# Lightning attention and a cosine FFN on one core: x produced transposed, state kept in PSUM with positional powers, FFN and attention interleaved in a fixed order

**Chip, cores, metric.** One core of one Trainium2 chip. The metric is the device time of one execution in microseconds (us), the median of several. The profile's span is some 1.7 us shorter than the device time of the same execution, so differences are taken within one of the two. The profiled execution of the kernel before is not among the three of its table: its span is 421.0. Lines with "..." mark cuts in code and in views.

## The reference

Two programs, one feeding the other. Attention with a decay lambda per head (4 batches, 8 heads, 768 positions, 64 features per head):

```python
for b in range(nb):                                   # blocks of 64 positions
    intra = (qb @ kb.T) * Dmask                       # Dmask[i,j] = lam**(i-j) for i >= j, else 0
    intra = intra @ vb
    inter = (qb * lam**(pos + 1)) @ kv_state
    out[block] = intra + inter
    kv_state = lam**block * kv_state + (kb * lam**(block-1-pos)).T @ vb
```

(That is the reference with its einsums written as products.) Then `x`, the output as 3072 tokens of 512 features, goes through an FFN with 2048 hidden features:

```python
h = x @ w_in
g = h * np.cos(h)
return (g @ w_out).astype(np.float32)
```

## The kernel before

It works in blocks of 128 tokens, 24 in all, and head by head. One head is a ring of small operations (cut to it):

```python
for h in range(H):
    ...
    ps_qkT = ps2_pool.tile([2 * D, BLK], BF16, tag="ps_qkT")
    nc.tensor.transpose(ps_qkT, qk_s[:, h, :, :], identb)
    ...
    nc.scalar.copy(q_b, ps_qkT[0:D, :])
    ...
    nc.vector.tensor_copy(k_b, ps_qkT[D:2 * D, :])
    ps_s = ps_pool.tile([BLK, BLK], F32, tag="ps_s")
    nc.tensor.matmul(ps_s, lhsT=k_b, rhs=q_b, start=True, stop=True)
    ...
    nc.vector.tensor_mul(s_masked, ps_s, dm_h)           # decay and causality in one mask per head
    ...
    nc.tensor.matmul(ps_o, lhsT=s_masked, rhs=v_sb, start=True, stop=first)
    if not first:
        nc.tensor.matmul(ps_o, lhsT=q_b, rhs=kv, start=False, stop=True)
    nc.scalar.copy(o_sb, ps_o)
    ...
    nc.tensor.matmul(ps_kv, lhsT=qk_s[:, h, 1, :], rhs=v_sb, start=True, stop=True)
    ...                                                  # new_kv = lam**128 * kv + ps_kv, two operations
nc.sync.dma_start(out=x_dram[r0:r0 + BLK, :], in_=o_all)
```

Only when attention is over does the FFN run, six tiles of 512 tokens, loading `x` back from memory and transposing it on PE:

```python
for t0 in range(0, N_TOK, T):
    for nt in range(NT):
        ...
        nc.sync.dma_start(out=x_tile, in_=x_dram[t0 + nt * 128:t0 + (nt + 1) * 128, :])
        for kd in range(KD):
            ...
            nc.tensor.transpose(ps_t, x_tile[:, kd * 128:(kd + 1) * 128], ident_bf)
            nc.scalar.copy(xT[:, kd, nt * 128:(nt + 1) * 128], ps_t)
    ...
    for f in range(KF):                                  # 16 slices of the hidden features
        ...                                              # 4 matmuls into ps_h, cosine on ACT, gate on DVE
        for nt in range(NT):                             # 4 matmuls that use the gate just made
            nc.tensor.matmul(out_ps[nt], lhsT=g[:, nt * 128:(nt + 1) * 128], rhs=w_out_sb[:, f, :], ...)
```

## Time and profile before

| | before |
|---|---|
| device time, median of 3 (range) | 419.84 (419.66 to 420.62) |
| span of the profile | 421.0 |
| busy: PE, DVE, ACT, POOL | 85%, 47%, 55%, 18% of the span |
| instructions | 6366 |
| first FFN matmul | 204.8 |

Added here is one turn of the attention's ring, from the timeline of the kernel before. Columns: start, length (us), engine, line, operation, output<-inputs, shapes; in brackets the idle time before it and what ended it.

```profile
60.56 0.23 DVE L136 COPY k_b<-ps_qkT 64x128 bf16<-64x128 bf16 x1
60.68 0.29 PE L139 MATMUL ps_s<-q_b,k_b 64*128 64x128 bf16 x1
61.01 0.29 DVE L141 TENSOR_TENSOR s_masked<-ps_s,dmaskT 128x128 bf16<-128x128 f32 x1 [0.23 <-PE ps_s L139]
```

Three operations of 0.23 to 0.29 us hand one head's 128x128 block from engine to engine. A matmul of 128 columns takes 0.29 us here because it is seen alone, from issue to landing. PE is "98% busy" in this stretch without ever streaming: the busy share of a latency-bound PE says little.

### The profile page before, as it was taken

The numbers are of one execution on the slowest core, as the hardware profiler recorded it, in microseconds if no ns is written. First come the engines' busy times: TensorE is split into PE (matmuls) and PEld (weight loads), VectorE is DVE, ScalarE is ACT, GpSimd is POOL, SyncE is SP. The second block draws the span as 40 slices with busy tenths as digits, with TensorE's granted clock in tenths as the row PEclk, the third lists the DMA queues.
The fourth block names the chain that finished last, engine by engine and source line by source line (L and its number), as shares of the span: only waits on it lengthen the run. The fifth ranks groups of instructions, "written<-read, shape, count | busy, mean of one in ns | idle before, by whom it ended". The sixth has DMA issues, their size and how long they took to land.

```text
span 421.0 us, 6366 instructions
## 1 busy us (share of the span) xinstructions
PE 356.0 (85%) x1792; PEld 169.1 (40%) x1792; DVE 196.4 (47%) x713; ACT 230.5 (55%) x796; POOL 75.3 (18%) x71
## 2 busy tenths in 40 slices
PE   0565999999999999994788888888888888888883
PEld 0232555555555555552334333433434343433331
DVE  4653777777777777773122323333232323232331
ACT  5544776777678767872633454363363445344323
POOL 5505643434343535200000000000000000000000
PEclk9999999999999999999999999999999999999998
DMA  9999947474647474201100030030011002002002
GB/s 165 214 194 227 213 107 158 106 159 102 138 101 160 104 154 111 62 19 47 50 14 12 13 126 12 12 114 26 12 64 63 25 19 107 15 0 100 0 2 100
DMA packets 88020, 36.07 MB, mean 86 GB/s; under 512 B 76208, under 2 KB 84400, under 8 KB 87984
## 3 DMA queue, kind: packets, MB, share of 16 engines
q1 hardware_dynamic: 85392, 31.47, 31.7%
q0 software_dynamic: 2592, 4.19, 5.4%
q8 instruction: 14, 0.23, 0.3%
q14 instruction: 22, 0.18, 0.1%
HBM read 30.41 MB, written 9.44 MB: 95 GB/s over the span
## 4 chain that ended last, share of the span: by engine, by line
PE 71%; ACT 9%; DVE 8%; issue 6%; POOL 3%; DMA 2%; ACTq 0%; SPq 0%; POOLq 0%
PE out_ps L192 22%; PE ps_h L185 11%; PE ps_qkT L132 9%; PE ps_o L145 9%; ACT cos_h L188 8%; PE ps_kv L152 8%; DVE g L190 8%; PE ps_o L147 6%; PE ps_s L139 5%; POOL qk_s L121 2%; DMA x_tile<-x_attn 1%; DMA lam_bc<-in_lam_dram 1%; PE ps_t L178 1%; DMA out_dram<-o_tile 0%; POOL dmaskT L80 0%
## 5 line engine op out<-in xcount | busy, mean ns | idle before, releaser
L190 DVE TENSOR_TENSOR g<-ps_h,cos_h 128x512 bf16<-128x512 f32 x96 | 66.4, 692 | 152.0 <-ACT cos_h L188 152.0
L188 ACT ACTIVATE cos_h<-ps_h,halfpi 128x512 f32<-128x512 f32 x96 | 66.0, 687 | 109.9 <-PE ps_h L185 109.8
L192 PE MATMUL out_ps<-w_out_sb,g 128*128 128x512 bf16 x384 | 100.5, 386 | 25.9 <-DVE g L190 25.9
L185 PE MATMUL ps_h<-xT,w_in_sb 128*128 128x512 bf16 x384 | 100.6, 386 | 0.0
L141 DVE TENSOR_TENSOR s_masked<-ps_s,dmaskT 128x128 bf16<-128x128 f32 x192 | 56.0, 292 | 49.8 <-PE ps_s L139 49.7
L132 PE MATMUL ps_qkT<-identb,qk_s 128*128 128x128 bf16 x192 | 55.0, 288 | 23.7 <-POOL qk_s L121 23.7
L134 ACT COPY q_b<-ps_qkT 64x128 bf16<-64x128 bf16 x192 | 49.6, 259 | 43.8 <-PE ps_qkT L132 27.8
L121 POOL TENSOR_TENSOR qk_s<-qk_f,qk_scale 128x1024 bf16<-128x1024 f32 x24 | 56.2, 2341 | 79.6 <-PE ps_kv L152 73.4
L192 PEld LDWEIGHTS <-g 128*128 128x128 bf16 x384 | 33.9, 99 | 72.8 <-DVE g L190 37.9
L185 PEld LDWEIGHTS <-w_in_sb 128*128 128x128 bf16 x384 | 38.1, 99 | 47.1 <-issue 3.2
L139 PE MATMUL ps_s<-q_b,k_b 64*128 64x128 bf16 x192 | 55.7, 290 | 0.1
L158 ACT ACTIVATE kv<-kv,lam_blk 64x64 bf16<-64x64 bf16 x160 | 55.5, 347 | 0.1
L152 PE MATMUL ps_kv<-v_all,qk_s 128*64 128x64 bf16 x192 | 49.9, 260 | 0.1
L149 ACT CAST o_all<-ps_o 128x64 bf16<-128x64 f32 x192 | 40.6, 211 | 12.6 <-PE ps_o L147 2.7
L145 PE MATMUL ps_o<-v_all,s_masked 128*128 128x64 bf16 x192 | 45.3, 236 | 1.5 <-DVE s_masked L141 1.2
L136 DVE COPY k_b<-ps_qkT 64x128 bf16<-64x128 bf16 x192 | 43.5, 226 | 6.3 <-ACT kv L158 0.2
L147 PE MATMUL ps_o<-kv,q_b 64*128 64x64 bf16 x160 | 37.1, 232 | 0.0
L152 PEld LDWEIGHTS <-qk_s 128*64 128x64 bf16 x192 | 24.2, 126 | 26.6 <-issue 0.2
L132 PEld LDWEIGHTS <-qk_s 128*128 128x128 bf16 x192 | 19.7, 103 | 36.0 <-POOL qk_s L121 23.8
L145 PEld LDWEIGHTS <-s_masked 128*128 128x128 bf16 x192 | 20.2, 105 | 32.4 <-DVE s_masked L141 32.3
L159 DVE TENSOR_TENSOR kv<-kv,ps_kv 64x64 bf16<-64x64 bf16 x160 | 32.4, 202 | 0.0
L179 ACT COPY xT<-ps_t 128x128 bf16<-128x128 bf16 x96 | 20.6, 268 | 6.8 <-PE ps_t L178 6.8
(37 smaller groups left out, 123.1 us busy)
## 6 DMA issues: line engine op xcount, KB each, us to landing
qk_f<-in_q_dram SPq DMA_DIRECT2D x24, 256.0 KB, 4.3
qk_f<-in_k_dram SPq DMA_DIRECT2D x24, 256.0 KB, 4.3
v_f<-in_v_dram SPq DMA_DIRECT2D x24, 256.0 KB, 4.0
out_dram<-o_tile SPq DMA_DIRECT2D x24, 256.0 KB, 2.0
x_attn<-o_all SPq DMA_DIRECT2D x24, 128.0 KB, 1.8
x_tile<-x_attn SPq DMA_DIRECT2D x24, 128.0 KB, 2.0
w_in_sb<-in_moe_w_in_dram POOLq DMA_DIRECT2D x1, 2048.0 KB, 14.2
w_out_sb<-in_moe_w_out_dram POOLq DMA_DIRECT2D x1, 2048.0 KB, 27.0
```

The source lines that it names most:

```text
L121: nc.gpsimd.tensor_mul(qk_s, qk_f, qk_scale)
L132: nc.tensor.transpose(ps_qkT, qk_s[:, h, :, :], identb)
L139: nc.tensor.matmul(ps_s, lhsT=k_b, rhs=q_b, start=True, stop=True)
L141: nc.vector.tensor_mul(s_masked, ps_s, dm_h)
L145: nc.tensor.matmul(ps_o, lhsT=s_masked, rhs=v_sb, start=True, stop=first)
L147: nc.tensor.matmul(ps_o, lhsT=q_b, rhs=kv, start=False, stop=True)
L152: nc.tensor.matmul(ps_kv, lhsT=qk_s[:, h, 1, :], rhs=v_sb, start=True, stop=True)
L158: nc.scalar.activation(new_kv, kv, AF.Copy, scale=lb_h[0:D, :])
L185: nc.tensor.matmul(ps_h, lhsT=w_in_sb[:, kd, f * 128:(f + 1) * 128], rhs=xT[:, kd, :], start=(kd == 0), stop=(kd == KD - 1))
L188: nc.scalar.activation(cos_h, ps_h, AF.Sin, bias=halfpi)
L190: nc.vector.tensor_mul(g, ps_h, cos_h)
L192: nc.tensor.matmul(out_ps[nt], lhsT=g[:, nt * 128:(nt + 1) * 128], rhs=w_out_sb[:, f, :], start=(f == 0), stop=(f == KF - 1))
```

## The change

The intent is that PE should have one continuous stream of work. Four things are done for it:

1. **Positional powers.** Rows of q are scaled by lambda^position and rows of v by lambda^-position, counted from the start of the batch. Then the mask is a plain triangle, the same for all heads, and the state needs no decay: it is a plain sum, left in one PSUM bank over the six blocks of a batch. (The lambdas of the test are 0.97 to 0.99, so lambda^-767 stays below 2e10; it grows as lambda falls.)
2. **Heads in pairs.** Two heads share each transpose (128 features), each score matmul (256 columns, q laid out block-diagonally) and each output; 8 heads' results move in one or two wide operations.
3. **x transposed on chip.** The value matmuls have their operands swapped, so that they give features x tokens, which the FFN reads as its `xT`. Two heads, each with v padded by zeros, add into one output. x is not stored or loaded.
4. **A fixed order.** Attention of tile i+1, first FFN matmuls of tile i and second FFN matmuls of tile i-1 share each of 16 slots of a stage; a block of attention is four slots.

The core of the diff, with cuts marked:

```diff
+    ctx.enter_context(tc.manual_schedule())
...
-                    nc.vector.tensor_mul(s_masked, ps_s, dm_h)
+        nc.vector.tensor_mul(s_m[n][:, 4 * half:4 * half + 4, :], sc.pop((n, half)),
+                             mask.unsqueeze(1).to_broadcast([P, 4, P]))
...
-                    nc.tensor.matmul(ps_o, lhsT=s_masked, rhs=v_sb, start=True, stop=first)
+        for p in range(NP):
+            if c:
+                nc.tensor.matmul(t[:, p, :], lhsT=kv_bd[(n - 1) % NK][:, p, :],
+                                 rhs=qkT[n][:, 0, p, :], start=True, stop=False)
+            for i in range(2):
+                nc.tensor.matmul(t[:, p, :], lhsT=v_pad[n % NV][:, 2 * p + i, :],
+                                 rhs=s_m[n][:, 2 * p + i, :],
+                                 start=(i == 0 and c == 0), stop=(i == 1))
...
-                        nc.scalar.activation(new_kv, kv, AF.Copy, scale=lb_h[0:D, :])
-                        nc.vector.tensor_add(new_kv, new_kv, ps_kv)
+            nc.tensor.matmul(kv_ps[:, p, :], lhsT=k_b[n][:, 2 * p:2 * p + 2, :],
+                             rhs=v_both(n, p), start=(c == 0 and p == 0), stop=True, ...)
...
-                nc.sync.dma_start(out=x_dram[r0:r0 + BLK, :], in_=o_all)
+        nc.scalar.copy(xT[i][:, :, j * P:(j + 1) * P], o_ps.pop(n))
...
+    for i in range(-1, NTILE + 1):
+        for s in range(KF):
+            ...                                    # weights in quarters, in stages -1 and 0
+            if 0 <= i < NTILE:
+                ffn_in(i, s)                       # 4 matmuls
+                ffn_cos(i, s)                      # ACT
+            after = None
+            if i + 1 < NTILE:
+                after = attend((i + 1) * NT + s // 4, s % 4)   # PE part of attention
+            if 0 <= i < NTILE:
+                ffn_gate(i, s)                     # DVE
+            if after:
+                after()                            # DVE or ACT part of attention
+            if i >= 1:
+                ffn_out(i - 1, s)                  # 4 matmuls
+                ffn_store(i - 1, s)
```

`attend` does the next block's transposes in slot 0, the first half of the scores and the state update in slot 1, the other half in slot 2, the values in slot 3.

## The prediction

> **What bounds the kernel now.** I read the windows view first, because the page averages over two programs run one after the other. Columns: the stretch, its length, busy time and instructions of PE, PEld, DVE, ACT, POOL, then clock, DMA share, GB/s.
>
> ```profile
> 15.00:34.00 19.00, 12.14 (x60) 6.13 (x60) 9.55 (x44) 9.28 (x40) 3.88 (x5) 1.00 1.16 200
> 34.00:196.00 162.00, 157.96 (x868) 81.58 (x868) 113.18 (x532) 117.20 (x504) 62.95 (x43) 1.00 0.57 122
> 196.00:205.00 9.00, 3.17 (x16) 1.54 (x17) 0.00 (x0) 3.04 (x14) 0.00 (x0) 1.00 0.25 78
> 205.00:414.00 209.00, 182.35 (x848) 79.90 (x847) 66.41 (x96) 91.46 (x200) 0.00 (x0) 1.00 0.11 38
> 414.00:421.00 7.00, 0.40 (x2) 0.00 (x0) 0.00 (x0) 2.04 (x4) 0.00 (x0) 0.84 0.40 150
> ```
>
> Some 34 us of start, 162 of attention, 9 of changeover, 209 of FFN, 7 of tail. Next the costliest groups, with the durations for pricing the change:
>
> ```profile
> L190 DVE TENSOR_TENSOR g<-ps_h,cos_h 128x512 bf16<-128x512 f32 x96 | 66.4, 692 | 152.0 <-ACT cos_h L188 152.0
> L188 ACT ACTIVATE cos_h<-ps_h,halfpi 128x512 f32<-128x512 f32 x96 | 66.0, 687 | 109.9 <-PE ps_h L185 109.8
> ...
> L192 PE MATMUL out_ps<-w_out_sb,g 128*128 128x512 bf16 x384 | 100.5, 386 | 25.9 <-DVE g L190 25.9
> ...
> L132 PE MATMUL ps_qkT<-identb,qk_s 128*128 128x128 bf16 x192 | 55.0, 288 | 23.7 <-POOL qk_s L121 23.7
> L134 ACT COPY q_b<-ps_qkT 64x128 bf16<-64x128 bf16 x192 | 49.6, 259 | 43.8 <-PE ps_qkT L132 27.8
> L121 POOL TENSOR_TENSOR qk_s<-qk_f,qk_scale 128x1024 bf16<-128x1024 f32 x24 | 56.2, 2341 | 79.6 <-PE ps_kv L152 73.4
> ```
>
> Attention does 192 heads; 162/192 is about 0.85 us each, through five short matmuls and six small ops in a ring of waits. PE shows 98% busy there, but these are latencies (288 ns for 128 columns), not streaming: a latency bound. FFN is different. The timeline there (start, length, what) shows one period of two hidden slices:
>
> ```profile
> 254.51 1.04 PE L192 MATMUL out_ps<-w_out_sb,g 128*128 128x512 bf16 x4 [0.53 <-DVE g L190]
> ...
> 256.47 1.67 PE L185 MATMUL ps_h<-xT,w_in_sb 128*128 128x512 bf16 x7
> 257.98 0.27 PE L178 MATMUL ps_t<-ident_bf,x_tile 128*128 128x128 bf16 x2
> 258.78 1.04 PE L192 MATMUL out_ps<-w_out_sb,g 128*128 128x512 bf16 x4 [0.53 <-DVE g L190]
> ```
>
> Period 4.27 us; 7 matmuls in 1.67 with the last 0.38 long give (1.67-0.38)/6 = 0.215 us each; 16 of them are 3.45, the rest is 0.53 of wait for the gate and two transposes. PE streaming bounds FFN, with about 19% lost. Last, how it enters FFN:
>
> ```profile
> 205.31 3.19 PE L185 MATMUL ps_h<-xT,w_in_sb 128*128 128x512 bf16 x7
> ```
>
> The same seven take 3.19: (3.19-0.63)/6 = 0.427 each, twice as long. So PE is at half rate after attention, although the granted-clock column says 1.00.
>
> **What the Trainium skill says.** (1) "TensorE: Matmul & The Clock Gate", section Wait — 56ns, not 53.3ns?: 512 columns cost 426.7 ns start to start cold and 215.7 warm; the trace agrees (427, 215). (2) The same page, Back-to-back issue gap, gives about 81 ns for a 128-column matmul in a stream with weight loads. No stream of these stands in this trace; I use 81 as an estimate, and 110 for 256 columns (256/512 of 216). (3) "VectorE: DVE Perf Modes", The TRN2 errata, gives (N+151)/0.96 ns for a two-tensor op: 691 at 512; the trace has 692. The perf-mode tier table lets a 16-bit copy out of PSUM go two per cycle and SBUF to SBUF four. The trace's copy of 128 bf16 columns out of PSUM, 226 ns, fits two per cycle plus 0.16 us. (4) "GPSIMD Engine Reference", Engine selection, says two-input ops are about twice as slow, one-input near line rate: the trace has 2341 ns for 1024 (2.29 per element) against 606 for 512 (1.18).
>
> **The change part by part.** *Removed*: x through memory (24 stores, 24 loads), 96 x transposes with 96 ACT copies (20.6 us of ACT), the changeover of 9 us, and the head-by-head ring. *PE work*: the 768 FFN matmuls stay: 768 x 0.2155 = 165.5 us. Attention per 128-token block: 8 transposes, 4 score matmuls of 256 columns, 4 state updates, up to 12 value matmuls: 24 x 0.081 + 4 x 0.11 = 2.4 us; 24 blocks 57. So PE has 223 us if it never waits.
> *DVE per block*: qkT copy of 1024 bf16 0.69; two q copies 0.29 each; two masks of 512 at 0.69; two state copies of 256 f32 at 0.41; sum 3.5. Four gates at 0.692 add 2.8: 6.3. *ACT*: 4 x 0.69 + 2 x 0.6 = 3.9. *POOL*: 512 x 2.29 = 1.17, a copy 0.61, two 256 multiplies 0.6 each: 3.0. In a full block all lie beside PE's 4 x (0.86+0.86) + 2.4 = 9.3.
>
> Stage by stage (a stage is 16 slots, four per block):
> - *Fill*, attention of tile 0 alone. lambda landed at 3.8 before; a table load and exponentials make scales at about 5.7; POOL delivers block 1's q and k at 10.6. Then a block costs what the chain costs with PE cold: transposes 1.05+0.15, qkT 1.27, masks and state 2.2, second half of values 0.8: 5.5. Block 0 starts at 10.6, four end at 33. DMA needs 5 blocks of 0.79 MB and three weight quarters of 0.52: 5.5 MB at the 203 GB/s of the start is 27 us, so just hidden. With the copy to xT and a little DMA delay: **35**.
> - *Stage 0*, first FFN matmuls plus attention. DVE and the fixed order set it. In a warm block, second-half values wait for gates 0 to 2 and both masks on DVE, which end 7.6 after the block starts, and half the value matmuls and latency follow: 8.25. Cold it is 10.9. I take a mix, 9 x 4: **36**.
> - *Stages 1 to 4*. Slot lengths 2.37, 2.26, 1.94, then values. A gate ends 2.77 after its slot's start (0.86 matmuls + 0.17 + 0.18 + 0.69 + 0.17 + 0.70). With DVE's order the second mask ends at 8.1, PE comes to it at 7.9: 0.3 of wait with latency. 9.6 x 16 blocks: **154**.
> - *Stage 5*, no attention: 128 x 0.2155 = **27.6**.
> - *Stage 6*, output only: 64 x 0.2155 = 13.8, plus three handovers of the single output bank at 0.9: **16.5**.
> - *Tail*: one copy, one store landing in 2.0, end: **4**, against 7.
> Sum 35+36+154+27.6+16.5+4 = **273 us**.
>
> **The rivals.** *A wait takes the removed one's place.* PE is in order, so a late mask stops FFN matmuls too. For it: DVE has 6.3 of 9.6 us, and the mask sits behind three gates. Against: keys and queries are transposed one block ahead, and half the value matmuls don't need that mask. If each block lost 1 us more, 16-20 us: 290. *Short matmuls pay for weight loads*: loads measure 99 to 126 ns. If each 128-column matmul takes 107 instead of 81, 24 x 26 ns x 24 blocks = 15 us: 288. If weight loads hide and they take 56, 14 us less: 259. *The start becomes memory-bound*: before, the third block's v came 15.1 us late behind both weight matrices (POOL waited for it). The weights now come in quarters after the first blocks, but the same bytes must land; 10 us worse is 283. *PE stays cold in stage 0*: its gaps may hold it there; 44 instead of 36 gives 281. *The transfers removed were hidden anyway*: true, x's memory traffic is worth only the 9 us changeover; the gain must come from overlap, not from bytes. None of these comes near 420: attention's 162 us has to reappear nearly whole for that.
>
> **Range and chances.** The errors above are up to about 15 either way, and partly cancel: 257 to 293. Even a sum of all bad cases, 273+18+15+10+8 = 324, is faster by over 20%. Faster 0.98, same 0.01, slower 0.01.
>
> **What would show it right or wrong.** In the changed trace: FFN matmuls at 215 ns and PE above 95% busy in the middle stages with about 38 us per stage; PE's largest waits in the mask (value matmuls) and small; stage 0 near 36 with DVE densest; first FFN matmul near 35; 128-column matmuls some 81 ns apart; POOL near 72 us in all. Wrong would be: middle stages above 42 us (a ring through DVE, or matmuls at 427 ns); the first FFN matmul after 45 (DMA); POOL ops much longer than priced because DVE's copies hold their shared way to SBUF; or PE gaps at every accumulator handover.

## The result

The changed kernel takes **253.17 us** (252.93 to 253.90, 4 runs), the kernel before beside it 420.23 (419.66 to 421.29, 4 runs). The ratio is **0.602** (95%: 0.6004 to 0.6038). Ratios are the mean time of one kernel's fast runs over that of the other's of the same rounds, so not quite the ratio of the medians. The direction was as predicted, but the time lies under the low end of the range, 257.

In the page of the kernel after, the chain that ended last (shares by engine), then the groups. Columns of a group: busy us, mean ns of one, idle us before it and what ended most of it:

```profile
PE 78%; DVE 13%; ACT 3%; DMA 2%; SPq 1%; issue 1%; POOL 0%; ACTq 0%
...
L212 DVE TENSOR_TENSOR g<-ps_h,cos_h 128x512 bf16<-128x512 f32 x96 | 66.4, 691 | 72.4 <-ACT cos_h L205 70.7
...
L199 PE MATMUL ps_h<-xT,w_in_sb 128*128 128x512 bf16 x384 | 99.8, 383 | 3.7 <-DVE g L212 2.4
L219 PE MATMUL ps_f<-w_out_sb,g 128*128 128x512 bf16 x384 | 96.6, 379 | 2.8 <-ACT o_sb L226 2.8
...
L162 PE MATMUL ps_o<-s_m,v_pad 128*128 128x128 bf16 x192 | 20.3, 227 | 13.8 <-DVE s_m L151 13.8
```

The gates and FFN matmuls are the same operations at the same durations as before. PE no longer waits 25.9 us for gates ahead of the second FFN matmuls. Its largest wait is the predicted one, the mask ahead of the value matmuls (13.8 us), so the next question is where that lies. The windows view of the kernel after (stretch, length, then busy us and instructions of PE, PEld, DVE, ACT, POOL, then clock, DMA share, GB/s):

```profile
0.00:33.50 33.50, 14.82 (x116) 11.83 (x117) 21.82 (x40) 5.53 (x10) 22.08 (x38) 0.95 1.18 204
33.50:64.60 31.10, 23.69 (x168) 13.60 (x168) 22.86 (x42) 14.60 (x21) 15.88 (x23) 0.95 1.20 213
...
64.60:202.16 137.56, 137.56 (x933) 76.32 (x933) 90.62 (x167) 61.68 (x95) 37.52 (x54) 1.00 0.45 100
```

In stages 1 to 4 PE is busy 137.56 of 137.56 us: the trace shows no wait there, and all of those 13.8 us lie before 64.6 us. The timeline of one middle block shows that this busy time really is streaming:

```profile
99.11 1.03 PE L199 MATMUL ps_h<-xT,w_in_sb 128*128 128x512 bf16 x4
99.97 0.39 PE L129 MATMUL ps_t<-ident,q_s 128*128 128x128 bf16 x4
100.19 0.39 PE L129 MATMUL ps_t<-ident,k_b 128*128 128x128 bf16 x4
100.42 1.03 PE L219 MATMUL ps_f<-w_out_sb,g 128*128 128x512 bf16 x4
...
100.89 0.69 DVE L212 TENSOR_TENSOR g<-ps_h,cos_h 128x512 bf16<-128x512 f32 x1 [1.71 <-ACT cos_h L205]
...
105.23 0.69 DVE L212 TENSOR_TENSOR g<-ps_h,cos_h 128x512 bf16<-128x512 f32 x1
...
105.84 0.68 DVE L151 TENSOR_TENSOR s_m<-ps_s,mask 128x512 bf16<-128x512 f32 x1
```

Read the starts, not the lengths. Eight transposes start at 99.97 and the next group at 100.42: 0.45/8 = 0.056 us each, though a lone one lasted 0.288 before. Four FFN matmuls take 99.97 - 99.11 = 0.86, so 0.215 each. On DVE, two operations of 0.69 start 0.61 apart.

| stage (us) | predicted | after | error |
|---|---|---|---|
| fill (attention of tile 0) | 35 | 33.5 | 1.5 |
| stage 0 | 36 | 31.1 | 4.9 |
| stages 1 to 4 | 154 | 137.6 | 16.4 |
| stage 5 (FFN only) | 27.6 | 27.8 | -0.2 |
| stage 6 (output only) | 16.5 | 17.3 | -0.8 |
| tail | 4 | 4.0 | 0.0 |
| sum | 273 | 251.2 (span) | 21.8 |

Three waits remain outside the middle, shown here from the timeline of the kernel after: at the start and the end of stage 0, and near the end of the kernel.

```profile
33.50 1.81 PE L199 MATMUL ps_h<-xT,w_in_sb 128*128 128x512 bf16 x4 [0.67 <-ACT xT L173]
...
63.49 0.27 PE L162 MATMUL ps_o<-s_m,v_pad 128*128 128x128 bf16 x2 [1.27 <-DVE s_m L151]
...
230.62 3.61 PE L219 MATMUL ps_f<-w_out_sb,g 128*128 128x512 bf16 x16 [0.68 <-ACT o_sb L226]
```

The first FFN matmuls run at half rate (1.81 us for four, 1.03 in the middle), value matmuls wait 1.27 us for the second mask, and each new output tile of the last stage waits 0.68 us until ACT has copied the single output bank. These three became experiments.

### The profile page after: what moved, and what is told of

Same layout as the page of the kernel before. It is cut to its first block, busy times and chain, and to the rows that moved or that the text cites. A ratio compares the mean times of both kernels' runs of the same rounds, so it can differ in the third digit from the quotient of the medians.

```text
span 251.2 us, 3773 instructions
## 1 busy us (share of the span) xinstructions
PE 218.3 (87%) x1408; PEld 120.4 (48%) x1408; DVE 146.4 (58%) x265; ACT 98.1 (39%) x150; POOL 75.5 (30%) x113
## 3 DMA queue, kind: packets, MB, share of 16 engines
q0 software_dynamic: 4224, 4.19, 10.6%
## 4 chain that ended last, share of the span: by engine, by line
PE 78%; DVE 13%; ACT 3%; DMA 2%; SPq 1%; issue 1%; POOL 0%; ACTq 0%
PE ps_f L219 33%; PE ps_h L199 30%; PE ps_o L162 4%; PE ps_t L129 4%; DVE s_m L151 4%; PE ps_s L144 3%; DVE g L212 3%; DVE q_bd L137 3%; DVE kv_bd L191 2%; DMA k_f<-in_k_dram 2%; DVE qkT L134 2%; PE ps_o L159 1%; PE ps_kv L179 1%; SPq L57 1%; ACT o_sb L226 1%; ACT cos_h L205 1%
## 5 line engine op out<-in xcount | busy, mean ns | idle before, releaser
L219 PE MATMUL ps_f<-w_out_sb,g 128*128 128x512 bf16 x384 | 96.6, 379 | 2.8 <-ACT o_sb L226 2.8
L219 PEld LDWEIGHTS <-g 128*128 128x128 bf16 x384 | 35.7, 98 | 34.3 <-issue 3.9
L117 POOL TENSOR_TENSOR q_s<-q_f,q_scale 128x512 bf16<-128x512 f32 x24 | 25.1, 1046 | 61.0 <-DMA q_f<-in_q_dram 57.5
L122 POOL TENSOR_TENSOR v_pad<-v_f,v_scale 128x256 bf16<-128x256 f32 x48 | 28.8, 621 | 29.3 <-PE ps_o L162 18.5
L151 DVE TENSOR_TENSOR s_m<-ps_s,mask 128x512 bf16<-128x512 f32 x48 | 32.7, 682 | 0.2
L162 PE MATMUL ps_o<-s_m,v_pad 128*128 128x128 bf16 x192 | 20.3, 227 | 13.8 <-DVE s_m L151 13.8
L173 ACT CAST xT<-ps_o 128x512 bf16<-128x512 f32 x24 | 14.1, 585 | 30.2 <-PE ps_o L162 30.2
L162 PEld LDWEIGHTS <-v_pad 128*128 128x128 bf16 x192 | 15.7, 102 | 18.6 <-issue 15.6
L144 PE MATMUL ps_s<-q_bd,qkT 128*128 128x256 bf16 x96 | 20.1, 294 | 0.0
L134 DVE COPY qkT<-ps_t 128x1024 bf16<-128x1024 bf16 x24 | 16.4, 682 | 5.7 <-PE ps_t L129 5.7
L137 DVE COPY q_bd<-qkT 64x512 bf16<-64x512 bf16 x48 | 18.0, 376 | 1.2
L191 DVE CAST kv_bd<-ps_kv 64x256 bf16<-64x256 f32 x40 | 16.7, 416 | 0.3
```

Source lines behind the costliest of these rows:

```text
L117: nc.gpsimd.tensor_mul(q_s[n], qf.pop(n), q_scale[:, c, :].unsqueeze(2).to_broadcast([P, H, D]))
L122: nc.gpsimd.tensor_mul(v_pad[n % NV][:, i::2, i * D:(i + 1) * D], v_n[:, i::2, :], v_scale[:, c, i::2].unsqueeze(2).to_broadcast([P, NP, D]))
L137: nc.vector.tensor_copy(q_bd[n % NQ][h, :, i, :], t[h, 0, :, :])
L144: nc.tensor.matmul(t[:, 2 * i:2 * i + 2, :], lhsT=qkT[n][:, 1, p, :], rhs=q_bd[n % NQ][:, p, :, :], start=True, stop=True)
L151: nc.vector.tensor_mul(s_m[n][:, 4 * half:4 * half + 4, :], sc.pop((n, half)), mask.unsqueeze(1).to_broadcast([P, 4, P]))
L162: nc.tensor.matmul(t[:, p, :], lhsT=v_pad[n % NV][:, 2 * p + i, :], rhs=s_m[n][:, 2 * p + i, :], start=(i == 0 and c == 0), stop=(i == 1))
```

## The experiments

Two questions. **Where does the gain come from?** My theory: mainly from the interleaving, since attention's latencies vanish under FFN matmuls; the other parts serve mostly to make that possible. The rival: attention in pairs of heads and x kept on chip are worth it by themselves, and the interleaving adds little; a second rival is that the scheduler would have found the order without being told. Runs 1 to 4 undo one part each. **Why was the prediction 20 us too long?** My theory: a 128-column matmul in a stream costs 0.056 us, not 0.081, and the wait for the mask does not occur. The rival: short matmuls do cost 0.081 and something else is faster than priced. Runs 5 to 7 add known work to each engine and read what it costs. Runs 8 to 12 remove the remaining waits. The texts say what each theory expected of each run. Runs of one group shared a chip with their runs of the kernel before; all gave correct results.

### 1. The scheduler's order (e1_auto)

```diff
-    ctx.enter_context(tc.manual_schedule())
```

> Only the line that fixes the order is taken out; the compiler's list scheduler then orders each engine (the same instructions, most of PE's and DVE's rows at other places). Theory A, the fixed order is a part of the gain: in the middle stages PE never waited (block period 8.68 us = 32 x 0.2157 + 1.78), and any other order puts a matmul in front of something that is ready, so I expect waits of 0.5 to 2 us per block, 262 to 290 us. Theory B, dependencies alone settle the time and the order is only cosmetic: 250 to 256 us.

Measured: 258.72 us, ratio 0.615 (0.612 to 0.617), 5.6 slower than after, between the ranges of the two theories. The loss is in the fill: the first FFN matmul comes at 41.1 instead of 33.5. Of these 7.6 us, 1.7 come back in stage 1 (32.8 against 34.5), and stages 2 to 4 are the same to within 0.1 us (34.5, 34.3, 34.1). The timeline of e1_auto (POOL) shows where:

```profile
15.72 0.80 POOL L103 DMA_DIRECT2D w_in_sb<-in_moe_w_in_dram  x1
...
26.66 1.03 POOL L117 TENSOR_TENSOR q_s<-q_f,q_scale 128x512 bf16<-128x512 f32 x1 [4.62 <-DMA q_f<-in_q_dram]
```

POOL waits 4.62 us for q, and PE's transposes wait 5.58 for POOL. The line at 15.72 is the last of the four quarters of `w_in`, all issued from 9.89 us on, where the fixed order spreads them from 15.66 to 31.15; the first quarter of `w_out` (needed only in stage 1) follows at 21.24. Counted by DMA packets, between 12 and 30 us the weights' queue moves 2.6 MB here against 1.4 after, and the queue of q, k and v 0.9 against 2.6. So the fixed order is worth about 5 us, and the trace puts them in the fill, where weight loads come ahead of q and k; no run moved those loads alone. In the steady state, given the program in this form, the scheduler's order does as well. Here the second rival was right about the middle and wrong about the start.

### 2. No interleaving (e2_no_interleave)

```diff
-    for i in range(-1, NTILE + 1):
+    for i in range(-1, NTILE - 1):
+        for s in range(KF):
+            attend((i + 1) * NT + s // 4, s % 4)()       # all attention first
+    for i in range(0, NTILE + 1):                        # then all of the FFN
...
-            xT[i] = work.tile([P, KD, T], BF16, tag="xT", name="xT")
+            xT[i] = work.tile([P, KD, T], BF16, tag="xT", name="xT", bufs=NTILE)
```

> All 24 blocks of attention first, then FFN with input of one tile beside output of the tile before; same instructions. Theory A, most of the gain over the kernel before is overlap: an attention block alone costs about 5.6 us as in the fill (transposes at 16.16, 21.95, 27.51), so 33 us + 20 x 5.6 = 145 at FFN's start, then 768 x 0.2157 = 166 plus about 12 of end waits, and 4 of tail: 325 us, 72 more than the changed kernel. Rival, the batching into pairs of heads is what counts and attention alone runs near its matmul price (1.8 to 3.8 us a block with the loads): 33 + 20 x 3.8 + 182 = 290 us or less.

Measured: 326.9 us (one slow run of 329.0 left out of the ratio), ratio 0.774 (0.768 to 0.779): 73.7 us slower than after, 93.5 faster than before. The windows view of e2_no_interleave, one stretch of attention and one of FFN:

```profile
33.00:137.00 104.00, 59.65 (x475) 48.20 (x473) 71.61 (x120) 10.49 (x18) 53.24 (x76) 0.61 0.88 158
...
175.00:320.00 145.00, 141.37 (x644) 64.13 (x656) 52.23 (x76) 64.40 (x97) 0.00 (x0) 1.00 0.11 41
```

Attention alone leaves PE idle for 43% of the time, and its clock at 0.61. It needs 5.5 us a block (19 blocks from 32.71 to 137.28 us) against 7.1 before (21 blocks from 36.24 to 184.88, by their first transposes); the FFN began at 204.8 then, at 145.1 here. FFN alone streams. So the gain of 169.8 us of span (421.0 to 251.2) divides in this order of steps: 59.7 because the FFN starts earlier, attention in its new form (pairs, powers, x kept on chip, with weights in quarters) taking less time and the changeover being gone; 35.8 because the FFN and the end after it (216.2 before, 180.4 here) lost their gate waits and x transposes; and 325.6 - 251.2 = 74.4 because attention is laid under the FFN. Both theories have a share; neither explains it alone. Within the first share pairs, powers and placement are not separated by this run.

### 3. The state decayed in SBUF (e3_state_in_sbuf)

```diff
-        c = n % NB
+        c = 0                                            # powers counted from the block's start
...
-                             rhs=v_both(n, p), start=(c == 0 and p == 0), stop=True,
+                             rhs=v_both(n, p), start=(p == 0), stop=True,
...
-            nc.vector.tensor_copy(kv_bd[n % NK][h, :, h], kv_ps[h, :, h])
+            ...                                          # acc = kv_ps, or acc + kv_ps
+            nc.vector.tensor_mul(acc[h, :, :], acc[h, :, :], dec...)    # dec = lam**128
+            nc.vector.tensor_copy(kv_bd[n % NK][h, :, h], acc[h, :, :])
```

> Positional powers and the sum in PSUM are undone: powers count within a block, the state is f32 in SBUF, scaled per block; six more DVE operations of 64 x 256 (about 0.4 us each, 2.2 us a block). Theory A (middle stages bound by PE, DVE has 11 us of slack in 34.5): the middle stages move little, only fill and first stage, where DVE sets the pace, get 8 x 1.5 to 2.2 us longer: 265 to 272. Rival (DVE's chain to the second mask is already as long as PE's path): every block pays about 2 us, 24 x 2 = 48: about 300 us.

Measured: 297.12 us, ratio 0.707 (0.703 to 0.710), 44 slower than after. (The text speaks of six more DVE operations; the edit has six where there were two, so four more.) Blocks with an update last 10.5 us, those without 8.46. The added operations last some 0.4 us each, and what stands behind them on DVE is late. The timeline of e3_state_in_sbuf:

```profile
141.00 1.10 DVE L201 CAST kv_bd<-acc 64x256 bf16<-64x256 f32 x1
...
143.97 0.68 DVE L155 TENSOR_TENSOR s_m<-ps_s,mask 128x512 bf16<-128x512 f32 x1
144.70 0.27 PE L166 MATMUL ps_o<-s_m,v_pad 128*128 128x128 bf16 x2 [2.04 <-DVE s_m L155]
```

PE waits for the second mask in each of the thirteen such blocks of stages 1 to 4, 1.23 to 2.40 us (median 1.71), which with the 8.68 of a block makes most of the 10.5 seen. By stages, of the 43.3 us that the span grew, the fill has 11.5, stage 0 has 7.6 and stages 1 to 4 have 24.3. So the first theory was right about fill and stage 0, where it expected 12 to 18, and fell in the middle stages, where it expected little (265 to 272 in all); there the rival was right: DVE was busy only two thirds of the middle stages (90.62 of 137.56 us), but the mask stands behind everything that the block gives to DVE. A share of busy time is not slack. The copy above took 1.10 us, the same one elsewhere in that stretch 0.29; here POOL was converting q and k beside it (from 140.92 on), so part of the loss may be this and not the added operations.

### 4. x through memory again (e4_x_through_memory)

```diff
-                nc.tensor.matmul(t[:, p, :], lhsT=v_pad[...], rhs=s_m[...], ...)
+                nc.tensor.matmul(t[:, p, :], lhsT=s_m[...], rhs=v_pad[...], ...)
...
-        nc.scalar.copy(xT[i][:, :, j * P:(j + 1) * P], o_ps.pop(n))
+        nc.scalar.copy(o_all, o_ps.pop(n))
+        nc.sync.dma_start(out=x_dram[n * P:(n + 1) * P, :], in_=o_all)
+        nc.sync.dma_start(out=x_tile, in_=x_dram[n * P:(n + 1) * P, :])
...                                                      # later: 4 transposes and an ACT copy to xT
```

> Attention gives x with tokens on partitions again, stored to memory, read back and transposed by PE (four 128-column matmuls a block), in the fixed order. Theory A (PE in order; x is needed at once by the next tile's first matmul): each of six tiles stops PE for copy 0.6 + store 2.0 + load 2.0 + transposes 0.4 + copy 0.6 = 5 to 6 us, less what the wait replaces, and 16 transposes per tile are 0.9 us: 253 + 6 x 6 = 285 to 295. Rival (the transfers hide behind the output matmuls of the last tile): 6 x 1 us, 260.

Measured: 320.18 us, ratio 0.761 (0.757 to 0.764), 67 slower than after, and more than I expected (285 to 295). Every fourth block lasts 14.3 to 14.9 us instead of 8.9. The timeline of e4_x_through_memory at such a place:

```profile
178.12 0.34 SPq L177 DMA_DIRECT2D x_attn<-o_all  x1
179.89 0.34 SPq L179 DMA_DIRECT2D x_tile<-x_attn  x1
182.00 0.61 PE L187 MATMUL ps_x<-ident,x_tile 128*128 128x128 bf16 x4 [3.88 <-DMA x_tile<-x_attn]
183.28 1.87 PE L214 MATMUL ps_h<-xT,w_in_sb 128*128 128x512 bf16 x4 [0.67 <-ACT xT L188]
```

The first FFN matmul of a tile needs the last block of attention, so the round trip, store, load, transpose and copy, stands in front of every tile: 3.88 + 0.67 us of stop, and then the matmuls run at half rate (four take 1.87 us instead of 1.03), which is one thing that I had left out. The other, larger one is the start: of the 66.6 us that the span grew, stages 1 to 4 have 29.8, but the fill has 22.4 (first FFN matmul at 55.9) and stage 0 has 12.8. There every block waits for its x, the last of the fill for 9.71 us (ended at 54.61): its store was issued at 45.59, the load back only at 52.38, while the weights still came in, and the next q, k and v only behind it, from 52.81 on. All of these are issued by SyncE in turn, so the run does not separate the round trip from loads held up behind it. The transfers removed are thus not hidden in this order, whereas the prediction's last rival held them hidden in the kernel before, but for 9 us. What a change is worth depends on the others beside it. The undone parts (73.7, 67, 44, 5.6) do not add up to the gain and are not meant to.

### 5. Eight more transposes per block (e5_pe_extra)

```diff
-                nc.tensor.transpose(t[:, i, p, :], src[:, 2 * p:2 * p + 2, :], ident)
+                for _ in range(2 if n > 8 else 1):
+                    nc.tensor.transpose(t[:, i, p, :], src[:, 2 * p:2 * p + 2, :], ident)
```

> Every transpose of blocks 9 to 23 is issued twice (same result): 15 x 8 = 120 more 128-column matmuls with their weight loads, nearly all in the middle stages. Theory A (PE is the bound there and a 128-column matmul costs 0.056 us): +6.7 us, 259.9. Rival 1, the price of the prediction (0.081): +9.7, 262.9. Rival 2 (a ring of waits is the bound, PE has room): +0 to 2.

Measured: 262.41 us, ratio 0.625 (0.622 to 0.627), 9.2 slower than after. Taken over some 15 blocks, that is 0.077 per extra matmul, close to the 0.081 of my prediction, and it would have misled me. The block period reads otherwise: 9.13 instead of 8.68, so 0.45/8 = 0.056. The timeline of e5_pe_extra agrees:

```profile
169.91 0.61 PE L130 MATMUL ps_t<-ident,q_s 128*128 128x128 bf16 x8
170.36 0.61 PE L130 MATMUL ps_t<-ident,k_b 128*128 128x128 bf16 x8
170.80 1.03 PE L220 MATMUL ps_f<-w_out_sb,g 128*128 128x512 bf16 x3
```

Sixteen from 169.91 to 170.80 are 0.056 each. (The last group shows 3 of its 4 matmuls; a record is missing.) The profiled execution was the slowest of the five (264.36 us). What it lost beyond 15 x 0.45 lies in stage 0, which took 35.3 us (32.39 to 67.68) instead of 31.1, and in the first block after it, both with stretches at half rate. **The disputed price is 0.056**, and a whole run's time, which the rival's 262.9 fits, was the wrong place to read it.

### 6 and 7. One more DVE operation, ahead of the mask or behind the values (e6_dve_before_mask, e7_dve_after_values)

```diff
# e6, slot 2                                  # extra(t): a 128x512 product like the mask's, result unused
-            return lambda: scores_out(n, 1)
+            return lambda: (n > 7 and extra(sc[n, 1]), scores_out(n, 1))
# e7, slot 3
-            return lambda: values_out(n)
+            return lambda: (values_out(n), n > 7 and extra(last[0]))
```

> One more DVE multiply of 128 x 512 (about 0.62 us start to start) per block of blocks 8 to 23, just ahead of the second mask. In the changed kernel the second mask of a middle block ends at 106.52 and PE comes to the value matmuls that need it at about 106.6. Theory A (PE bound, but the mask only just makes it): the slack is about 0.1 us, so each block waits about 0.5: +8 us, 261. Rival (there is ample slack): +0 to 1.

> The same multiply, the same number of times, but in the slot of the value matmuls, after the gate. Theory A (DVE idles there, busy 23 of 34.5 us in a stage): +0 to 0.5 us, 253.5. Rival (DVE's total work counts): the same +8 us as ahead of the mask.

Measured: ahead of the mask 262.65 us (ratio 0.625), behind the values 255.19 (0.605). In the middle blocks: 9.20 and 8.68 against 8.68 after. The same operation costs 0.52 us a block in one place and nothing in the other. The timeline of e6_dve_before_mask has the wait in the value matmuls:

```profile
111.58 0.38 PE L167 MATMUL ps_o<-s_m,v_pad 128*128 128x128 bf16 x4 [0.53 <-DVE s_m L151]
```

An operation adds 0.61 us to DVE's stream (the spacing seen above), of which 0.52 reaches PE, so the second mask had about 0.09 us to spare. The predicted danger was real, and my 0.3 us of wait missed the border by less than 0.4 us. The 2 us that e7 lost all the same lie outside the middle blocks: stage 0, in which it has no added operation, took 32.1 us (33.37 to 65.43) instead of 31.1, and the first block of stage 1 lasted 10.4. Two of its five executions took 253.4 and 253.6.

**A half-rate window.** Runs 5 to 8 share an oddity: the first block of stage 1 takes 10.4 to 10.9 us instead of 8.68 (in runs 5 and 6 with 0.45 and 0.52 of their own). The recorded clock changes only in windows of 3.41 us, and only between full and half. I compared PE's busy time in each window with the rate in the next one. Windows view of e8_q_from_psum, the window at the end of stage 0 and the one after it:

```profile
60.50:63.90 3.40, 1.39 (x12) 0.73 (x10) 1.91 (x4) 1.03 (x2) 0.91 (x2) 1.00 0.99 218
63.90:67.30 3.40, 3.40 (x16) 1.75 (x15) 2.04 (x4) 0.69 (x1) 2.21 (x4) 0.50 0.80 171
```

And the corresponding window of the kernel after, which kept the full rate:

```profile
60.90:64.31 3.41, 1.76 (x16) 1.04 (x16) 3.09 (x6) 1.03 (x2) 1.96 (x3) 1.00 1.13 231
```

Busy 1.39 of 3.40 (41%) lost the next window; 1.76 of 3.41 (52%) kept it. Over all thirteen traces (after and the twelve experiments, from 25 us on, the end of each kernel left out), every full-rate window followed by a half-rate one had PE busy 43% or less, and those that stayed full had 46% or more, but for one of 42%. Before 25 us two windows lost the full rate at 44% and 47%, so the border is not sharp. To come back took more: below 74% none did, from 74% to 83% some, and from 84% on all. This is a regularity of the records, with PE's busy time partly modelled and, in runs 1 to 8, a few matmul records missing; no run varied it on purpose. It would explain why waits at the end of stage 0 cost about 1.5 us in some profiles and nothing in others: it depends on how the window falls on them.

### 8. q copied from PSUM (e8_q_from_psum)

```diff
-        nc.vector.tensor_copy(t, tr.pop(n))
+        src = tr.pop(n)
+        nc.vector.tensor_copy(t, src)
...
-            nc.vector.tensor_copy(q_bd[n % NQ][h, :, i, :], t[h, 0, :, :])
+            nc.vector.tensor_copy(q_bd[n % NQ][h, :, i, :], src[h, 0, :, :])
```

> The two block-diagonal q copies read the transposes in PSUM instead of their copy in SBUF. In the fill they took 1.0 to 1.9 us a pair while POOL was busy, and 0.59 where it was not; out of PSUM I expect 0.8 to 0.9 a pair always. Theory A (DVE and POOL share a way to SBUF in these copies, and DVE sets the fill): fill and first stage 2 to 4 us shorter, middle stages unchanged: 249 to 251.5. Rival (the long copies had other reasons, or the fill hangs on loads): 253 to 255, as each pair costs 0.25 us more.

In the fill, the copies of q to its block-diagonal place vary widely (shortest/median/longest ns, then the stretch of their starts). Kernel after:

```profile
L137 DVE COPY q_bd<-qkT x10: 291/651/1130, 8.5 to 29.8; 64x512 bf16<-64x512 bf16 x10
```

The same in e8_q_from_psum, from PSUM instead of SBUF:

```profile
L138 DVE COPY q_bd<-ps_t x10: 405/416/428, 8.4 to 27.4; 64x512 bf16<-64x512 bf16 x10
```

From SBUF a copy takes 291 ns at best and up to 1130 in the stretch where POOL is busiest; from PSUM it is slower at best and always the same. Over the whole trace of the kernel after, the 34 of these copies that overlap no operation of POOL last 284 to 292 ns, and all nine that last over 300 overlap one; in e8 the 18 that overlap one last 405 to 429, like the others (406 to 428). So POOL's work beside it stretches the copy from SBUF and not the one from PSUM. The fill shortened by 2.1 us (33.5 to 31.4), as expected. The total did not: 253.0 us, ratio 0.601 (0.598 to 0.604), because in the profiled execution 1.7 us went to the half-rate window above and 0.5 to stage 0 itself. The five executions run from 250.73 to 254.25. The change was right, and in the profiled execution its gain was eaten one stage later.

### 9. PE kept warm (e9_warm_pe)

```diff
+    def spin(k):                                   # on zeros, into the output bank, not yet in use
+        for _ in range(k):
+            nc.tensor.matmul(ps_idle, lhsT=idle[:, 0:P], rhs=idle, start=True, stop=True)
...                                                 # 14 before and 4 after the first transposes,
...                                                 # 10 per block of tile 0, 4 per block of tile 1,
...                                                 # before and amid the value matmuls
```

> PE is kept busy where it waits: 14 matmuls of 512 columns on zeros before the first transposes, 4 after them, 6 and 4 inside the value matmuls of the first four blocks, 4 inside those of the next four, all into a bank that is free then. Theory A (PE runs at half rate in the fill, and falls back to it for a 3.4 us window once or twice in the first FFN stage, because it idles there): transposes and values of the fill take half as long, the first FFN matmuls 1.03 instead of 1.81 and 1.55 us, and no window of half rate in stage 0: fill 31 to 32 us, stage 0 29 to 31, total 247 to 251. Rival (DVE's chain and the loads set both stages, PE's rate doesn't matter): 253 to 256, as the spinning delays real matmuls a little.

Measured: 251.46 us, ratio 0.5985 (0.596 to 0.601), just above the 247 to 251 expected. The clock is at full rate from 6.9 us to the end, the first FFN matmul starts at 30.9 instead of 33.5, and its group of four takes 1.02 us instead of 1.81. Stage 0 gave back 0.65, which fits idle matmuls that take PE's time where it is not waiting. The median is 1.7 us under after's in another round; the ratios' intervals (0.596 to 0.601 and 0.600 to 0.604) just touch.

### 10. The second mask ahead of the gate (e10_mask_first)

```diff
+            if after and s % 4 == 2:
+                after()
             if 0 <= i < NTILE:
                 ffn_gate(i, s)
-            if after:
+            if after and s % 4 != 2:
                 after()
```

> In the slot of the second mask, DVE does the mask ahead of the gate. Theory A (one more DVE operation ahead of the mask cost 0.52 us a block, so the slack is under 0.1; this gives 0.6 more, but a middle block is bound by PE at 8.68): middle stages unchanged at 34.5, stage 0 shorter by 4 x 0.6 = 2.4, total 250 to 252. Rival (the gate, now later, stops the matmuls two slots on): middle blocks over 8.8 us, 255 or more.

Measured: 252.01 us (one slow run of 256.43 left out of the ratio), ratio 0.5985 (0.597 to 0.600). Stage 0 went from 31.1 to 30.2, not the 2.4 shorter that I expected: moving the mask forward makes the gate later, and PE's waits in stage 0 for masks fell from 4.3 to 2.2 us while those for gates rose from 2.4 to 2.8 and those for xT from 0.7 to 1.3. The middle stages did not move, as they must not if PE is the bound there.

### 11. Two banks for the last stage (e11_two_banks)

```diff
+            if i == NTILE - 1 and j % 2:
+                f_out[i] = ps_1.tile([P, DM], F32, tag="ps_o", name="ps_f")   # attention's, free by then
+            else:
                 f_out[i] = ps_1.tile([P, DM], F32, tag="ps_f", name="ps_f")
```

> In the last stage the output tiles alternate between their bank and the one of the attention output, which is free then. Theory A: three of the four handovers of 0.7 us at the end go: -2.1 us, 251. Rival (something else follows just behind, the copy or the store): within 0.5 us of 253.2.

Measured: 251.6 us, ratio 0.598 (0.5955 to 0.601). This median stands between two groups: three executions took 250.1 to 250.3, three 252.9 to 253.3; the profiled one is of the first. In the timeline of e11_two_banks the last 64 matmuls are one group:

```profile
230.58 13.97 PE L222 MATMUL ps_f<-w_out_sb,g 128*128 128x512 bf16 x64 [0.67 <-ACT o_sb L229]
```

13.97 us is 64 x 0.2155 and the last one's latency; the waits of 0.68 between output tiles are gone, and the last copy starts at 244.63 instead of 247.26, 2.6 earlier, where 2.1 was expected.

### 12. All four together (e12_best)

Runs 8, 9 (with 2 idle matmuls per block of tile 1 in place of 4), 10 and 11 in one kernel.

> The kept-busy PE (with 2 in place of 4 in the second four blocks), the mask ahead of the gate, two banks at the end and q out of PSUM together. If the parts add: 253.2 - 3 (PE at full rate) - 2.4 (mask) - 2.1 (banks) - 2 (q in the fill) = 243.7; 242 to 247. If fill and stage 0 are set by loads instead, the first and the last part give nothing: 248 to 250.

Measured: **244.91 us** (244.85 to 245.37), ratio 0.582 (0.581 to 0.583): faster than both kernels, 3.3% under the kernel after by the medians (244.91/253.17). Windows view of e12_best, fill and stage 0:

```profile
0.00:29.81 29.81, 24.70 (x175) 13.74 (x176) 19.20 (x41) 5.53 (x10) 18.51 (x33) 1.00 1.16 201
29.81:59.30 29.49, 24.54 (x176) 13.67 (x176) 23.17 (x42) 14.58 (x21) 14.97 (x23) 1.00 1.09 198
```

The fill is 3.7 shorter than after's and stage 0 1.6, with the clock at 1.00 throughout; the end gives the rest of the 8.1 us of span. Singly these edits had brought 0.2 to 1.7 us of the median, 4.6 in all, and together 8.3. My explanation is that singly a gain in the fill can be lost to a half-rate window, and with PE kept at full rate that loss no longer occurs. This fits, but it is not shown: no run without only the idle matmuls was made.

## Why the prediction was wrong

The mechanism was right in the main: PE's stream bounds stages 1 to 4 (run 5), DVE sets most of stage 0 (its operations are some 60% of that stage's critical chain), the fill is a chain with PE cold (run 9), and overlap is the largest of three shares of the gain (run 2). Fill, stage 5, stage 6 and tail were within 1.5 us each. In the fill that is partly luck: its four blocks take 23.9 us (9.58 to 33.50) where 22 was priced, most copies of q lasting 0.57 to 1.13 us instead of 0.29, and an earlier start (10.6 was predicted) and the 2 us set aside for the last copy and DMA delay made up for it. The terms that were mis-sized:

- **"I use 81 as an estimate"**, the price of a 128-column matmul in a stream, failed and is the largest term. Runs show 0.056 (the transposes of a middle block, and run 5). With it a block is 32 x 0.2157 + 24 x 0.0557 + 4 x 0.109 = 6.90 + 1.34 + 0.44 = 8.68, which is the period measured. Over 16 middle blocks, 24 x 0.0253 x 16 = 9.7 us of the 16.4.
- **"0.3 of wait with latency"** in each middle block failed: PE never waits there. The gate was said to end 2.77 after its slot's start and ends 101.58 - 99.11 = 2.47 after it (the gate of 100.89 lasts 0.69): I had added the hand-over latency on top of durations that contain it, and took DVE's operations as 0.69 apart where they follow at 0.61. That is 4.8 us. Run 6 shows how near it was: 0.09 us of slack.
- Not counted at all: the first block of a batch has no state matmuls and the last no update, 4 matmuls or 0.22 us fewer, five times in these stages: 1.1 us. The very last block has no next one to transpose, 8 matmuls or 0.45 us fewer (it lasts 8.01). Rounding (9.56 to 9.6, 153.6 to 154) is another 1.0. These terms sum to 17.1; of the 0.7 too many, most is that the FFN matmuls of a block take 6.90 where 6.88 was priced, and that stages 2 and 3 are each 0.09 longer than the sum.
- **"Cold it is 10.9. I take a mix, 9 x 4: 36"** failed by 4.9 us. The blocks of stage 0 took 8.46, 6.54, 7.83 and 8.26 us: PE was at full rate from 37.0 us on, 3.5 us into the stage, and the same over-long DVE terms are in the warm figure. The 6.54 is block 5, the last of a batch, which has no update and no state copies; the prediction priced four full blocks.
- The rivals: **"If weight loads hide and they take 56, 14 us less: 259"** is what happened, and it was written down. The range failed because its low end of 257 left room for that alone; with stage 0 and the wait erring the same way the sum was 251. I had said that the errors "partly cancel", but the large terms leaned one way: an operation in a stream was priced too long, for PE by the 81 of a page that no stream in the trace could check, for DVE by what a lone operation takes.
- The other rivals: no wait took the removed one's place in the middle (run 3 shows how one would); the start did not cost the 10 us more that were feared of memory (POOL's longest wait for a load is 2.21 us in the fill and 5.86 in stage 0; run 1 shows what it costs when loads come late); PE at half rate held in stage 0 for its first 3.5 us only. A reading without consequence: "162/192" counts 24 blocks, but two were done before 34 us, and the blocks of attention before are 7.1 us apart, 0.88 a head.

## What to carry to other kernels

Price a pipelined operation by the distance of the starts in a dense stretch, and an added latency only once; when several terms of a sum share an assumption, let the range lean with it. An engine with a third of its time free may still have no slack at one position: put one extra operation there and look. Read what a part costs from the period of its stage, since a run's total mixes it with what later stages give back.

## What the Trainium skill lacked or had wrong

- "TensorE: Matmul & The Clock Gate", Back-to-back issue gap, gives about 81 ns per 128-column and about 131 ns per 512-column matmul as sustained with weight loads, and calls 56 and 216 the isolated figures. The runs show 56 and 216 in a stream that loads weights before every matmul (block of 8.68 us; 8 more transposes add 0.45).
- The same page, Why this matters for your kernels, ties the loss of full rate to an idle gap of over some 3 us; elsewhere it tells of frequent short idles with the same effect, without a figure. Here windows of 3.41 us in which PE was still busy up to 43%, in two traces up to 47%, lost it, in several short waits of at most 1.3 us (e8_q_from_psum: busy 1.39 of 3.40), and nearly all of 46% and more kept it. What share of a window is enough stands nowhere.
- "VectorE: DVE Perf Modes", The TRN2 errata: the duration of a two-tensor operation is right (691 ns), but operations that follow each other start 0.61 us apart (0.598 to 0.609 behind 59 gates of the kernel after), a distance for which it gives no figure.
- No page: the clock's record begins with its first change, so half rate before it shows as 1.00 (first FFN matmuls of the kernel before 0.427 us apart from 205.31 us on under a granted clock of 1.00; first record of the kernel before at 213.91 us, of the kernel after at 23.35).
